# V28 in the rows of w_o, V27 and K31: one ring tile, another layout of w_down's last rows and a copy in three pieces

## The chip, the cores and the metric

The kernel runs on one core of a Trainium2 chip. The metric is the device time of one execution in microseconds (us); the median over runs is given, and one further execution was profiled. The core has engines that work side by side and meet only at semaphores: PE (TensorE, matrix products; its weight loads are listed as PEld), DVE (VectorE), ACT (ScalarE), POOL (GpSimd) and SP (SyncE, which here issues the loads). Loads from memory run on 16 DMA engines. A load is issued by SP, carries 128 rows, one for each partition of the on-chip memory (SBUF), and its semaphore is counted up when all of it has landed. PE writes to PSUM.

## The reference, cut to what matters

One decoding step with two tokens (B = 2), D = 512. The token is normalized; attention over a window of the last W = 2048 cached positions with 32 heads of 128, and a bilinear gated layer with F = 1376 hidden columns, are added to it:

```python
def _A_ref(x, k_cache, v_cache, wq, wo):
    W = min(4096, max(256, Sk // 4))                       # 2048
    q = (x @ wq).reshape(B, Sq, Hq, Dh)                    # 32 heads of 128
    k, v = k_cache[:, :, Sk - W:, :], v_cache[:, :, Sk - W:, :]
    p = softmax(einsum("bhqd,bhkd->bhqk", q, k) * Dh ** -0.5)
    return einsum("bhqk,bhkd->bhqd", p, v).reshape(B, Sq, Hq * Dh) @ wo

def _B_ref(x, w_gate, w_up, w_down):
    return ((x @ w_gate) * (x @ w_up)) @ w_down

xn = layernorm(x)
return x + _A_ref(xn, ...) + _B_ref(xn, ...)
```

All of it is float32. Each head has its own keys and values, so every byte of the cache window is used once: 32 heads times 2 MB of keys and 2 MB of values, and 25 MB of weights.

## The kernel before, in words

**Layout.** The 2 x 2048 positions of a head are put on 128 partitions (64 for each token), 32 positions each, so the keys of one head are a field of 128 rows of 4096 words (CK, 16 KB a row, 2048 KB in all), and so are its values. The host lays all fields out in one DRAM stream (`laid_out`), in the order in which they are loaded, and each load of `loads()` is one contiguous piece of it with 128 equal rows.

**Groups.** Heads are worked in NG = 8 groups of HG = 4. In iteration `it` the keys of group `it` and the values of group `it - 1` are worked. Group g has three loads: `g.0` (two keys and V of head 4g-4), `g.1` (one key, two V) and `g.2` (w_o's rows of the group before, one V, one key, the next columns of w_q). The loads `g.0`, `g.1` and `g.2` are counted on three semaphores, B0, B1 and B2. Group 0's loads carry the gate, up and part of the w_down weights in the place of V. Behind the last keys come `8.0` (V28), `8.1` (V29, V30), `8.2` (V31), `wo` (w_o's last rows), and `d0`, `d1`, `d2` (w_down's rows). The last key is K31 in `7.2`, which also carries V27 and w_o's rows of group 6.

**Ring.** The loads go into three SBUF tiles (`ring`, widths `TILES`), with a fixed slot for each kind of field (`PLACES`), and a field overwrites the one before it in its slot. `Program.put` finds from the overlapping ranges what an instruction has to wait for, so the load of a field waits for the last reader of what it overwrites. SP issues the loads strictly in the order of the program: a load that waits holds those behind it.

**An iteration.** PE: gather of the group before (`gather`), the query columns (`project`), the spread of the maxima (`spread`, tile `top`), w_o's products (`wo`, into `acc`), then the weighing of four heads (`weigh`, eight products each, into `o_ps`), each behind the load with its V. DVE: for each of four keys a product with the query (`products`) and sums over the head's 128 columns (`sums`), then the maxima, the differences and the denominators. ACT: the exponentials (`weights`, tile `p`) and the copies of `o_ps` to `o_sb`, in two halves, with the semaphores `fold` and `fold2`, for which `gather` waits. PE's instructions stand in a loop whose body is run for all groups; that is why its waits are counts that grow with the iteration (`hold`).

**The tail.** After the last group: `scaled` and `wo` for group 7, the four `ROWS` of w_down (from `d0`) into `acc`; DVE adds the token's row (`acc_sb`); the `STRIPS` of w_down (7 and 8 from `d1`, 9 from `d2`) go into `acc_g` in groups of 128 columns, `add_groups(id4, acc_sb)` adds the rest to them, and DVE copies the result to `o_out`, which SP stores. w_down has 1376 = 10 x 128 + 96 rows; chunk NFC = 10, its last 96 rows, is padded to 128 rows of 512 columns, and worked with the chunks 0, 5 and 6 (`EARLY`) in group 0.

Of the kernel before, what the change touches and what calls it, by code (L numbers as in the profile page):

```python
# [10 lines left out]
P = 128  # L11
# [18 lines left out]
EARLY, ROWS, STRIPS = (0, 5, 6, NFC), (1, 2, 3, 4), (7, 8, 9)  # L30
# [5 lines left out]
def gu_cols(n):  # L36
# [18 lines left out]
def field_at(kind, i):  # L55
    if kind == "wq":
        return PLACES["wq", 0][0], C_WQ + i[1] * FB
    if kind == "wo":
        return 2, i % HG * CO
    if kind == "c":  # L60
        return 2, C_C
    return PLACES[kind, i % HG]


def loads():
# [34 lines left out]
    for name, ids in (("d0", ROWS), ("d1", STRIPS[:-1]), ("d2", STRIPS[-1:])):  # L100
        out[name] = (None, [wd[i] for i in ids])
# [3 lines left out]
def placed():  # L105
# [3 lines left out]
    for name, (_, fields) in loads().items():  # L109
        at, lo, tile = None, None, None  # L110
        for kind, i in fields:
            w = gu_cols(i[2]) if kind == "gu" else WIDTHS[kind]
            if kind == "gu":
                t, c = tile, at
            elif kind == "wd":
                if at is not None:
                    t, c = tile, at
                elif name == "0.2":
                    t, c = 2, HG * CO + CK - len(EARLY) * CO
                else:  # L120
                    t, c = 0, (ROWS + STRIPS).index(i) * CO
            else:
                t, c = field_at(kind, i)
            assert at is None or (t, c) == (tile, at), (name, kind, i, c, at)
            got[kind, i] = (t, c, w)
            lo = c if lo is None else lo
            tile, at = t, c + w
        assert at <= TILES[tile], (name, at)
        spans[name] = (tile, lo, at)
    return got, spans  # L130

# [23 lines left out]
class Program:  # L155
# [74 lines left out]
    def plan(self, looped):  # L230
# [46 lines left out]
        for i, o in enumerate(ops):  # L277
            if o.dma:
# [8 lines left out]
    def emit(self, looped, control):  # L287
# [10 lines left out]
        def give(i, first=None):  # L298
# [10 lines left out]
            if i in at:  # L309
                ins.then_inc(sem[o.tag], 16 if o.dma else 1)  # L310
# [127 lines left out]
def build(nc, stream, x_nat, out):  # L438
    pr = Program(nc)
    pe, dve, act, pool = pr.pe, pr.dve, pr.act, pr.pool  # L440

    ring = [pr.sb(f"step{i}", [P, w]) for i, w in enumerate(TILES)]
    xr = pr.sb("xr", [P, D])
    ones = pr.sb("ones", [P, P])
# [19 lines left out]
    hT = pr.sb("hT", [P, 4, NFB, B])  # L464
    acc_sb = pr.sb("acc_sb", [P, D])
# [12 lines left out]
    got = {key: ring[t][:, c : c + w] for key, (t, c, w) in where.items()}  # L478
    src, pos, tag_of = {}, 0, {}
    for name, (tag, _) in loads().items():  # L480
        t, lo, hi = spans[name]
# [4 lines left out]
    def issue(name):  # L486
        t, lo, hi = spans[name]
        pr.load("SP", ring[t][:, lo:hi], src[name], tag=tag_of[name])
# [352 lines left out]
```

## Time and profile before

| what | value |
|---|---|
| median of 3 runs | 376.26 us (376.07 to 377.44) |
| profiled execution | 375.96 us, span 374.6 us |
| DVE busy | 299.5 us (80% of the span) |
| PE busy | 177.2 us (47%), mean granted clock 0.718 |
| ACT, POOL busy | 18.3 us, 3.0 us |
| moved by DMA | 159.62 MB, mean 426 GB/s over the span |
| loads issued on SP | 20 of 6144 KB, 12 others |

The span goes from the first instruction to the last. Nearly every instruction has the line L139 (the helper that records operations), so rows are told apart by their tiles: `step` is the ring, `o_ps` the weighed values, `gu` the PSUM tile that also takes the gather, `q` the query tile, which at the end takes `acc_g`. PE's float32 products show up as two records each, so a head's eight weighing products are counted as x16.

### The profile page before, as it was taken

How to read it: one execution, taken by the hardware profiler on the slowest of the kernel's cores; microseconds unless marked ns; L12 is line 12 of the kernel's file. 1: busy time of each engine (PE TensorE's matmuls, PEld its weight loads, DVE VectorE, ACT ScalarE, POOL GpSimd, SP SyncE). 2: the span in 40 equal slices, each digit the busy share in tenths (PEclk: the TensorE clock that was granted, in tenths of full speed). 3: DMA queues.
4: the chain of work that ended last, by engine and by line, in shares of the span. 5: the costliest groups of instructions: out<-in, count | busy, mean ns of one | idle time of the engine just before them, and what ended most of it. 6: DMA issues, size and time to landing. Idle time of an engine off the chain costs nothing.

```text
span 374.6 us, 2080 instructions
## 1 busy us (share of the span) xinstructions
PE 177.2 (47%) x850; PEld 54.9 (15%) x850; DVE 299.5 (80%) x151; ACT 18.3 (5%) x42; POOL 3.0 (1%) x16
## 2 busy tenths in 40 slices
PE   0664743337516184073923277061740645334876
PEld 0210121002101030010400032010300112010322
DVE  0089999998599796997699975997969976999911
ACT  4000200000000000000000000000000000000000
POOL 3000000000000000000000000000000000000000
PEclk9965859587855688565695858567965659656899
DMA  9999999999999999999999999999999999989996
GB/s 365 415 457 408 444 420 420 457 467 420 420 420 420 430 493 420 420 420 420 425 462 457 420 420 420 420 441 483 420 420 420 420 425 472 446 382 431 439 411 275
DMA packets 4756, 159.62 MB, mean 426 GB/s; under 512 B 530, under 2 KB 658, under 8 KB 916
## 3 DMA queue, kind: packets, MB, share of 16 engines
q1 hardware_dynamic: 4752, 159.62, 98.9%
q10 hardware_dynamic: 4, 0.00, 0.0%
HBM read 159.55 MB, written 0.07 MB: 426 GB/s over the span
## 4 chain that ended last, share of the span: by engine, by line
DMA 50%; DVE 47%; PE 2%; issue 0%; SPq 0%; DVEq 0%
DMA step<-in_stream_dram 50%; DVE step L139 23%; DVE s L139 22%; PE q L139 2%; DVE rs L139 1%; SPq L139 0%; PE acc L139 0%; DVE h_sb L139 0%; PE top L139 0%; DVE nm L139 0%; DVE o_out L139 0%; DVE mt L139 0%; DVE dg L139 0%; DVE mtt L139 0%; DVE mc L139 0%
## 5 line engine op out<-in xcount | busy, mean ns | idle before, releaser
L139 DVE TENSOR_TENSOR step<-step,q 128x4096 f32<-128x4096 f32 x32 | 141.3, 4416 | 41.2 <-DMA step<-in_stream_dram 41.2
L139 PE MATMUL o_ps<-step,p 128*32 128x512 f32 x512 | 93.7, 884 | 156.2 <-DMA step<-in_stream_dram 153.7
L139 DVE TENSOR_REDUCE s<-step 128x32 f32<-128x4096 f32 x32 | 141.4, 4418 | 0.8
L139 PEld LDWEIGHTS o_ps<-step,p 128*32 128x32 f32 x512 | 18.7, 147 | 218.4 <-DMA step<-in_stream_dram 170.6
L139 PE MATMUL q<-step,xnb 128*128 128x512 f32 x72 | 42.0, 736 | 9.0 <-DVE step L139 6.3
L139 PEld LDWEIGHTS q<-step,xnb 128*128 128x128 f32 x72 | 16.5, 241 | 28.2 <-issue 18.2
L139 PE MATMUL gu<-step,xn 128*2 128x512 f32 (+1 forms) x48 | 14.8, 786 | 11.4 <-DMA step<-in_stream_dram 11.4
L139 ACT COPY o_sb<-o_ps 128x256 f32<-128x256 f32 x16 | 5.2, 375 | 247.3 <-PE o_ps L139 247.3
L139 PE MATMUL gu<-step,o_sb 128*128 128x8 f32 x64 | 10.1, 285 | 4.0 <-ACT o_sb L139 4.0
L139 PEld LDWEIGHTS gu<-step,o_sb 128*128 128x128 f32 x64 | 9.4, 225 | 16.5 <-ACT o_sb L139 16.5
L139 ACT ACTIVATE p<-s,zero 64x128 f32<-64x128 f32 x16 | 6.4, 399 | 63.5 <-DVE s L139 63.4
L139 PE MATMUL acc<-step,oT 128*2 128x512 f32 x64 | 8.3, 592 | 0.4 <-DVE oT L139 0.4
L139 DVE TENSOR_REDUCE nm<-top 64x4 f32<-64x8 f32 x16 | 2.6, 164 | 7.0 <-PE top L139 6.9
L139 DVE RECIPROCAL rec<-tot 128x8 f32<-128x8 f32 x8 | 1.6, 199 | 6.2 <-PE tot L139 6.2
L139 PEld LDWEIGHTS gu<-step,xn 128*2 128x2 f32 x48 | 2.9, 99 | 23.2 <-DMA step<-in_stream_dram 13.1
L139 PE MATMUL top<-dg,ones 128*128 128x16 f32 x16 | 2.9, 258 | 6.6 <-DVE dg L139 6.6
L139 DVE TENSOR_REDUCE st<-xc 128x4 f32<-128x16 f32 x1 | 0.2, 169 | 6.2 <-POOL xc L139 6.2
L139 DVE TENSOR_TENSOR oT<-gu,rec 128x8 f32<-128x8 f32 x8 | 1.3, 157 | 4.3 <-PE gu L139 4.3
L139 PEld LDWEIGHTS top<-dg,ones 128*128 128x128 f32 x16 | 2.5, 188 | 12.5 <-DVE dg L139 11.4
L139 DVE TENSOR_REDUCE rs<-p 128x8 f32<-128x256 f32 x8 | 3.3, 414 | 0.9 <-ACT p L139 0.9
L139 ACT ACT_TABLE_LOAD x3 | 3.8, 1283 | 3.1 <-POOL xr L139 3.1
L139 PE MATMUL top<-st,mean_w 128*128 128x4 f32 x2 | 0.6, 364 | 6.4 <-DVE st L139 6.4
(44 smaller groups left out, 31.9 us busy)
## 6 DMA issues: line engine op xcount, KB each, us to landing
step<-in_stream_dram SPq DMA_DIRECT2D x20, 6144.0 KB, 30.4
step<-in_stream_dram SPq DMA_DIRECT2D x2, 4096.0 KB, 23.7
step<-in_stream_dram SPq DMA_DIRECT2D x1, 6080.0 KB, 18.8
step<-in_stream_dram SPq DMA_DIRECT2D x1, 5568.0 KB, 31.5
step<-in_stream_dram SPq DMA_DIRECT2D x1, 5120.0 KB, 29.8
step<-in_stream_dram SPq DMA_DIRECT2D x2, 2048.0 KB, 22.0
step<-in_stream_dram SPq DMA_DIRECT2D x2, 1024.0 KB, 11.6
step<-in_stream_dram SPq DMA_DIRECT2D x1, 1057.0 KB, 4.9
```

Of the source, the lines that this page charges most:

```text
L139: return getattr(engine, self.method)(*self.args, **self.kw)
```

## The change

1. **One ring tile.** The three tiles become one, `step`, of 36992 words a partition, and the slots are ordered anew: V1, V2, K2; w_q, w_o, V3, K3, V0, K0, K1 (the numbers are those within a group). Each load's fields stand in the order of the slots.
2. **V28 in `7.2`.** In the new order V0's slot follows K3's, so `7.2` is extended by V28: its rows are w_o's rows of group 6, V27, K31 and V28 (14336 words instead of 10240). `8.0` is gone. As V28's slot holds V24 until that is weighed, the issue of `7.2` moves behind `weigh(vs[0])` of iteration 7. The count on B0 that `8.0` gave is given by a memset on POOL that waits for `7.2`.
3. **w_down.** Chunk 10 becomes 128 rows of 384 columns: 96 rows as they are, and below them the last 128 columns of these rows as 32 rows of three pieces. It moves to the `STRIPS` (in `d1`, with chunk 8), chunk 7 takes its place in `EARLY`. `rest()` works it: three pairs of products, one with 96 rows and one with 32, the latter with `h3`, to which ACT copies the hidden columns in group 0.
4. **Copies in three pieces.** `o_ps` is copied to `o_sb` in 128, 128 and 256 columns, with three semaphores, and `gather` waits for each before the product that reads it.

The diff, cut to its core:

```diff
@@ -27,7 +27,8 @@
 M = 4 * N
 CK, CO, CQ = J * DH, D, HG * DH
 CX = B * NC + 4 * N + 4 * HG + 2 * NFB + 2 + B
-EARLY, ROWS, STRIPS = (0, 5, 6, NFC), (1, 2, 3, 4), (7, 8, 9)
+EARLY, ROWS, STRIPS = (0, 5, 6, 7), (1, 2, 3, 4), (NFC, 8, 9)
+REST = 3 * P
 GU = [(w, c, n) for w in range(2) for c in range(NC) for n in range(NFB)]
 GU_A = [(0, c, n) for c in range(NC) for n in (2, 0)] + [(0, 0, 1)]
 GU_B = [t for t in GU if t not in GU_A]
@@ -41,25 +42,37 @@
 
 
 
+
+C_WQ = 3 * CK + P
+C_WO = C_WQ + NC * FB
+C_V3 = C_WO + HG * CO
+C_K3 = C_V3 + CK
+C_V0 = C_K3 + CK
+C_K0 = C_V0 + CK
+RING = C_K0 + 2 * CK
 PLACES = {
-    ("k", 0): (0, 0), ("k", 1): (0, CK), ("v", 0): (0, 2 * CK),
-    ("k", 2): (1, 0), ("v", 1): (1, CK), ("v", 2): (1, 2 * CK),
-    ("wo", 0): (2, 0), ("v", 3): (2, HG * CO), ("k", 3): (2, HG * CO + CK),
-    ("wq", 0): (2, HG * CO + 2 * CK),
+    ("v", 1): 0, ("v", 2): CK, ("k", 2): 2 * CK,
+    ("v", 3): C_V3, ("k", 3): C_K3, ("v", 0): C_V0,
+    ("k", 0): C_K0, ("k", 1): C_K0 + CK,
 }
-C_WQ = HG * CO + 2 * CK
-C_C = C_WQ + NC * FB
-TILES = (3 * CK, 3 * CK, C_C + CX)
 
 
 def field_at(kind, i):
     if kind == "wq":
-        return PLACES["wq", 0][0], C_WQ + i[1] * FB
+        return C_WQ + i[1] * FB
     if kind == "wo":
-        return 2, i % HG * CO
+        return C_WO + i % HG * CO
     if kind == "c":
-        return 2, C_C
+        return C_WQ - CX
+    if (kind, i) == ("k", HG - 1):
+        return C_V3
     return PLACES[kind, i % HG]
+
+
+def width(kind, i):
+    if kind == "gu":
+        return gu_cols(i[2])
+    return REST if (kind, i) == ("wd", NFC) else WIDTHS[kind]
 
 
 def loads():
@@ -72,33 +85,33 @@
         return [("v", h) for h in ids]
 
     def wq(g):
-        return [("wq", (g, c)) for c in range(NC)]
+        return [("wq", (g, c)) for c in range(NC)] if g < NG else []
 
     def wo(g):
         return [("wo", h) for h in range(g * HG, g * HG + HG)]
 
+    def wd(*ids):
+        return [("wd", i) for i in ids]
+
     gu_a, gu_b = [("gu", t) for t in GU_A], [("gu", t) for t in GU_B]
-    wd = {i: ("wd", i) for i in range(NFC + 1)}
     out = {
-        "x": ("B2", wq(0) + [("c", 0)]),
-        "0.0": ("B0", k(0, 1) + gu_a),
-        "0.1": ("B1", k(2) + gu_b),
-        "0.2": ("B2", [wd[i] for i in EARLY] + k(3) + wq(1)),
+        "x": ("B2", [("c", 0)] + wq(0)),
+        "0.0": ("B0", gu_a + k(0, 1)),
+        "0.1": ("B1", gu_b + k(2)),
+        "0.2": ("B2", wq(1) + wd(*EARLY) + k(3)),
     }
     for g in range(1, NG):
         a, b = g * HG, g * HG - HG
-        out[f"{g}.0"] = ("B0", k(a, a + 1) + v(b))
-        out[f"{g}.1"] = ("B1", k(a + 2) + v(b + 1, b + 2))
-        out[f"{g}.2"] = (
-            "B2", wo(g - 1) + v(b + 3) + k(a + 3) + (wq(g + 1) if g + 1 < NG else [])
-        )
+        out[f"{g}.0"] = ("B0", v(b) + k(a, a + 1))
+        out[f"{g}.1"] = ("B1", v(b + 1, b + 2) + k(a + 2))
+        out[f"{g}.2"] = ("B2", wq(g + 1) + wo(g - 1) + v(b + 3) + k(a + 3))
     b = H - HG
-    out[f"{NG}.0"] = ("B0", v(b))
+    out[f"{NG - 1}.2"][1].extend(v(b))
     out[f"{NG}.1"] = ("B1", v(b + 1, b + 2))
     out[f"{NG}.2"] = ("B2", v(b + 3))
     out["wo"] = (None, wo(NG - 1))
     for name, ids in (("d0", ROWS), ("d1", STRIPS[:-1]), ("d2", STRIPS[-1:])):
-        out[name] = (None, [wd[i] for i in ids])
+        out[name] = (None, wd(*ids))
     return out
 
 
...
@@ -275,7 +284,7 @@
         places = {ops[j].place for j in wanted if ops[j].eng == "PE" and ops[j].tag == "PE"}
         at, value = {}, {}
         for i, o in enumerate(ops):
-            if o.dma:
+            if o.dma or o.tag in PARTS:
                 step = 16
             elif o.tag in self.tags or i in wanted or (o.eng == "PE" and o.place in places):
                 step = 1
@@ -307,7 +316,7 @@
             if w:
                 ins._wait_ge(*w[-1])
             if i in at:
-                ins.then_inc(sem[o.tag], 16 if o.dma else 1)
+                ins.then_inc(sem[o.tag], 16 if o.dma or o.tag in PARTS else 1)
 
         sections = {}
         for i, o in enumerate(ops):
@@ -439,8 +448,9 @@
     pr = Program(nc)
     pe, dve, act, pool = pr.pe, pr.dve, pr.act, pr.pool
 
-    ring = [pr.sb(f"step{i}", [P, w]) for i, w in enumerate(TILES)]
+    ring = pr.sb("step", [P, RING])
     xr = pr.sb("xr", [P, D])
+    none = pr.sb("none", [P, 1])
     ones = pr.sb("ones", [P, P])
     mean_w = pr.sb("mean_w", [P, P])
     eps_t = pr.sb("eps", [P, 1])
...
@@ -613,10 +624,9 @@
 
     def gather(g):
         pr.part("g")
-        pr.hold("fold", g + 3, "r")
         for r in range(4):
-            if r == 2:
-                pr.hold("fold2", g + 3, "r")
+            if r < 3:
+                pr.hold(f"fold{r}", g + 3, "r")
             pe.matmul(
                 pk_ps[:, 0:N], o_sb[:, r * DH : (r + 1) * DH], pick[:, r, :],
                 start=(r == 0), stop=(r == 3),
@@ -640,8 +650,22 @@
         n_grp += 1
 
     def down(c, add, *args, **kw):
-        k = min(P, F - c * P)
-        add(hT[:k, c % 4, c // 4, :], got["wd", c][:k], *args, **kw)
+        add(hT[:, c % 4, c // 4, :], got["wd", c], *args, **kw)
+
+    def rest():
+        nonlocal n_grp
+        k, w = F - NFC * P, got["wd", NFC]
+        for j in range(3):
+            part = slice(j * P, (j + 1) * P)
+            pe.matmul(
+                acc_g[32 * j : 32 * j + B, :], hT[:k, NFC % 4, NFC // 4, :], w[:k, part],
+                start=(n_grp == 0), stop=False,
+            )
+            pe.matmul(
+                acc_g[96 : 96 + B, :], h3[k:, j, :], w[k:, part],
+                start=(n_grp == 0 and j == 0), stop=False,
+            )
+        n_grp += 1
 
     def wo(g):
         pr.part("o")
...
@@ -691,9 +715,9 @@
             weights(g)
             if it >= 2:
                 wo(g - 1)
-        if it < NG:
+        if it < NG - 1:
             issue(f"{it}.2")
-        else:
+        elif it == NG:
             for name in ("wo", "d0", "d1", "d2"):
                 issue(name)
         ks = [it * HG + hh for hh in range(HG)] if it < NG else []
@@ -703,6 +727,10 @@
             pr.hold("p", it + 1, "r")
             pr.hold("B0", it + 1, "r16")
             weigh(vs[0])
+        if it == NG - 1:
+            issue(f"{it}.2")
+            pr.also = [got["v", H - HG]]
+            pool.memset(none, 0.0, tag="B0")
         if ks:
             products(ks[0])
         if vs:
@@ -711,7 +739,8 @@
             sums(ks[0])
             products(ks[1])
             sums(ks[1])
-            issue(f"{it + 1}.0")
+            if it < NG - 1:
+                issue(f"{it + 1}.0")
         if vs:
             pr.hold("B1", it + 1, "r16")
             weigh(vs[1])
@@ -728,6 +757,10 @@
             sums(ks[2])
             if it == 0:
                 act.copy(hT.rearrange("p i n b -> p (i n b)"), hT_ps[:, 0 : 4 * B * NFB])
+                n = (NFC % 4 * NFB + NFC // 4) * B
+                for j in range(3):
+                    act.copy(h3[96:, j, :], hT_ps[32 * j : 32 * j + 32, n : n + B],
+                             tag=f"fold{j}" if j else None)
                 pr.section, pr.step = "gu", len(GU) + 4
                 for j, i in enumerate(EARLY):
                     down(i, add_rows, j, first=True)
@@ -735,8 +768,8 @@
         if vs:
             pr.hold("B2", it + 2, "r16")
             weigh(vs[3])
-            for n, half in enumerate((slice(0, FB // 2), slice(FB // 2, FB))):
-                act.copy(o_sb[:, half], o_ps[:, half], tag=("fold", "fold2")[n])
+            for n, part in enumerate((slice(0, P), slice(P, 2 * P), slice(2 * P, FB))):
+                act.copy(o_sb[:, part], o_ps[:, part], tag=f"fold{n}")
         if it == NG - 1:
             issue(f"{NG}.2")
         if ks:
@@ -750,7 +783,7 @@
         down(i, add_rows, j, last=True)
     dve.tensor_tensor(acc_sb, acc, xr, op=ALU.add)
     for i in STRIPS[:-1]:
-        down(i, add_groups)
+        rest() if i == NFC else down(i, add_groups)
     add_groups(id4, acc_sb)
     down(STRIPS[-1], add_groups, last=True)
     dve.tensor_copy(o_out, acc_g)
@@ -802,7 +835,12 @@
         if kind == "wo":
             return wo[i]
         if kind == "wd":
-            return np.pad(wd[i * P : (i + 1) * P], ((0, max(0, (i + 1) * P - F)), (0, 0)))
+            if i < NFC:
+                return wd[i * P : (i + 1) * P]
+            w = wd[i * P :]
+            return np.concatenate(
+                [w[:, :REST], w[:, REST:].reshape(3, 32, P).transpose(1, 0, 2).reshape(32, REST)]
+            )
         w, c, n = i
         return gu[w][:, c, n * FB : min(n * FB + FB, F)]
 
```

More of the change, by code (lines that the diff above doesn't have):

```diff
@@ L109, in placed @@
     for name, (_, fields) in loads().items():
[L110 to L119, printed above, removed]
-                else:
[L121 to L129, printed above, removed]
+        fixed = [n for n, (kind, _) in enumerate(fields) if kind not in ("gu", "wd")]
+        if fixed:
+            at = field_at(*fields[fixed[0]]) - sum(width(*f) for f in fields[: fixed[0]])
+        else:
+            late = ROWS + STRIPS
+            at = C_K0 + sum(width("wd", i) for i in late[: late.index(fields[0][1])])
+        lo = at
+        for n, (kind, i) in enumerate(fields):
+            assert n not in fixed or at == field_at(kind, i), (name, kind, i, at)
+            got[kind, i] = (at, width(kind, i))
+            at += width(kind, i)
+        assert at <= RING, (name, at)
+        spans[name] = (lo, at)
     return got, spans
+PARTS = ("B0", "B1", "B2")
 class Op:
@@ L477, in build @@
     where, spans = placed()
-    got = {key: ring[t][:, c : c + w] for key, (t, c, w) in where.items()}
+    got = {key: ring[:, c : c + w] for key, (c, w) in where.items()}
     src, pos, tag_of = {}, 0, {}
     for name, (tag, _) in loads().items():
-        t, lo, hi = spans[name]
+        lo, hi = spans[name]
         src[name] = stream[pos : pos + P * (hi - lo)].rearrange("(p i) -> p i", p=P)
@@ L514, in build @@
         act.activation(t, ones[:, 0:1].to_broadcast([P, FB]), AF.Copy, scale=0.0,
-                       tag="fold" if t is acc else "fold2")
+                       tag=f"fold{(acc, *gu_ps).index(t)}")
     xd, sq = xc[:, 0], xc[:, 1]
```

10 lines of the change are left out of this document (5 added, 5 removed).

## The prediction, made before the changed kernel was run

> **What bounds the kernel now.** I read the page first, then the timeline of the last 60 us, then the DMA issues and stages of the granted clock. The page says which resource is full:
>
> ```profile
> span 374.6 us, 2080 instructions
> q1 hardware_dynamic: 4752, 159.62, 98.9%
> ```
>
> One queue keeps the 16 DMA engines busy for 98.9% of the span, so up to the last group the transfers set the pace, and an edit off that queue costs nothing there. The end is another stage. In the timeline below (start, duration, engine, operation; in brackets the idle time before it and what ended it) each row ended by a DMA gives the landing of one load.
>
> ```profile
> 315.89 6.83 SPq L139 DMA_DIRECT2D step<-in_stream_dram  x2
> 319.01 4.42 DVE L139 TENSOR_TENSOR step<-step,q 128x4096 f32<-128x4096 f32 x1 [3.44 <-DMA step<-in_stream_dram]
> 319.03 3.30 PE L139 MATMUL o_ps<-step,p 128*32 128x512 f32 x16 [3.20 <-DMA step<-in_stream_dram]
> 333.56 0.20 PEld L139 LDWEIGHTS o_ps<-step,p 128*32 128x32 f32 x8 [12.62 <-DMA step<-in_stream_dram]
> ...
> 345.56 0.20 DVE L139 RECIPROCAL rec<-tot 128x8 f32<-128x8 f32 x1
> 345.68 4.42 DVE L139 TENSOR_TENSOR step<-step,q 128x4096 f32<-128x4096 f32 x1
> 345.69 0.20 PEld L139 LDWEIGHTS o_ps<-step,p 128*32 128x32 f32 x8 [5.64 <-DMA step<-in_stream_dram]
> ...
> 350.13 4.42 DVE L139 TENSOR_REDUCE s<-step 128x32 f32<-128x4096 f32 x1
> 350.73 3.68 PE L139 MATMUL q<-step,xnb 128*128 128x512 f32 x8
> ...
> 355.66 0.40 PE L139 MATMUL top<-dg,ones 128*128 128x16 f32 x2 [1.26 <-DVE dg L139]
> 355.99 1.04 PE L139 MATMUL acc<-step,oT 128*2 128x512 f32 x8
> ...
> 356.80 0.81 ACT L139 ACTIVATE p<-s,zero 64x128 f32<-64x128 f32 x2 [6.76 <-DVE s L139]
> ...
> 357.72 0.19 PEld L139 LDWEIGHTS o_ps<-step,p 128*32 128x32 f32 x8 [1.63 <-issue]
> 357.75 1.92 PE L139 MATMUL o_ps<-step,p 128*32 128x512 f32 x16 [0.72 <-ACT p L139]
> 360.29 0.16 PEld L139 LDWEIGHTS o_ps<-step,p 128*32 128x32 f32 x8 [1.52 <-DMA step<-in_stream_dram]
> 360.30 3.64 PE L139 MATMUL o_ps<-step,p 128*32 128x512 f32 x32 [0.62 <-DMA step<-in_stream_dram]
> 360.75 0.13 PEld L139 LDWEIGHTS o_ps<-step,p 128*32 128x32 f32 x4 [0.30 <-issue]
> 361.18 0.13 PEld L139 LDWEIGHTS o_ps<-step,p 128*32 128x32 f32 x4 [0.30 <-issue]
> ...
> 363.86 0.30 PEld L139 LDWEIGHTS tot<-rs,ones 128*128 128x128 f32 x2 [0.84 <-issue]
> ...
> 365.20 1.92 PE L139 MATMUL o_ps<-step,p 128*32 128x512 f32 x16 [0.94 <-DMA step<-in_stream_dram]
> ...
> 367.19 0.65 ACT L139 COPY o_sb<-o_ps 128x256 f32<-128x256 f32 x2 [9.58 <-PE o_ps L139]
> 367.61 1.06 PE L139 MATMUL gu<-step,o_sb 128*128 128x8 f32 x8 [0.49 <-ACT o_sb L139]
> ...
> 369.03 1.04 PE L139 MATMUL acc<-step,oT 128*2 128x512 f32 x8 [0.36 <-DVE oT L139]
> 370.18 1.04 PE L139 MATMUL acc<-step,hT 128*2 128x512 f32 x8
> 371.29 0.69 DVE L139 TENSOR_TENSOR acc_sb<-acc,xr 128x512 f32<-128x512 f32 x1 [2.31 <-PE acc L139]
> 371.46 0.62 PE L139 MATMUL q<-step,hT 128*2 128x128 f32 x16 [0.24 <-DMA step<-in_stream_dram]
> ...
> 372.72 0.29 DVE L139 COPY o_out<-q 128x128 f32<-128x128 f32 x1 [0.74 <-PE q L139]
> ```
>
> Read it as landings: 7.0 at 319.03 (V24 with K28, K29), 7.1 at 333.56, 7.2 at 345.69 (K31, V27), 8.1 at 360.29 (V29, V30), 8.2 at 365.20 (V31). V28 (8.0) shows no waiter: its bytes lie between 345.69 and 360.29. The one tie that matters is at 345.68. DVE had worked without a stop since 319 and finished its `rec` at 345.76; the load with K31 landed in the same tenth. From there runs the last compute chain: product K31, its sums, maxima, `top`, Exp, weighing V28 at 357.75, V29 and V30, V31, gather, w_o, the sum and the store. Only in its PE part does it wait for loads.
>
> **The change part by part.**
>
> *V28 in load 7.2.* Rows of 40 KB become rows of 56 KB, and 8.0 goes. DVE's product of K31 waits for the whole load, so it now waits for V28's 2048 KB also. Sizes (count, KB each, us from issue to landing):
>
> ```profile
> step<-in_stream_dram SPq DMA_DIRECT2D x20, 6144.0 KB, 30.4
> ...
> step<-in_stream_dram SPq DMA_DIRECT2D x1, 5120.0 KB, 29.8
> ...
> step<-in_stream_dram SPq DMA_DIRECT2D x1, 1057.0 KB, 4.9
> ```
>
> Let r be the time of 1024 KB and f what a load costs beside its bytes. 7.1: f + 6r = 333.56 - 319.03 = 14.53. 7.2: f + 5r = 12.13. 8.0 with 8.1: 2f + 6r = 14.60. 8.2: f + 2r = 365.20 - 360.29 = 4.91. The first two give r = 2.40, the others f of 0.07 to 0.11. V28 therefore adds 2r = 4.80, and K31 lands at 350.5 instead of 345.69. DVE has nothing else: everything behind that product on its queue (sums of K31, oT, maxima, weights) is late with it. Bounds 4.7 to 4.9 (a third of 14.60 is 4.87). I take **+4.80**.
>
> [...]
>
> *The issue of 7.2 moves behind the weighing of V24*, whose slot it overwrites. SP issued 7.2 at 315.89 and then stood for 8.0; now 7.2 goes out when the weighing ends, 319.03 + 3.30 = 322.33. The engines are then busy with 7.1 until 333.56: 11 us of cover. Behind it on SP stand 8.1, 8.2, w_o's last rows and the w_down loads. 8.2 waits for V27's weighing, 4.8 late, about 354; 8.1 keeps the engines until about 360. w_o's rows wait for the w_o products of the group before, 357.03 + 4.8 = 361.8, with 8.2 in flight until about 365. No hole is left, **0**; one of 2 us would still lie ahead of where PE now needs these rows.
>
> *POOL's memset that signals B0* runs once 7.2 has landed, at 350.5, with nothing behind it on POOL. PE asks for it at 362.5: **0**. Without those 12 us of cover it would be its own duration, about the 0.10 of this row:
>
> ```profile
> 2.41 0.10 POOL L139 MEMSET zero<- 128x1 f32 x1
> ```
>
> *What the late chain no longer waits for.* Shifted by 4.8, weighing V28 starts at 362.55. V29, V30 have landed and V31 lands during it. Weight loads go 0.43 apart per four (360.75, 361.18), so 16 take 1.71: V29's could have begun at 357.72 + 1.71 = 359.43 and began at 360.29, a wait of 0.86; V31's could have begun 0.30 after `tot`'s at 363.86, a wait of about 1.03. PE's own brackets say 0.62 + 0.94 = 1.56. Between 1.56 and 1.89 I take **-1.75**. w_down's first rows came 0.11 late too (369.03 + 1.04 = 370.07 against 370.18): **-0.11**.
>
> *Copies in three pieces.* By form, the ACT rows are:
>
> ```profile
> L139 ACT COPY o_sb<-o_ps 128x256 f32<-128x256 f32 x16 | 5.2, 375 | 247.3 <-PE o_ps L139 247.3
> L139 ACT COPY hT<-gu 128x24 f32<-128x24 f32 x1 | 0.2, 180 | 4.9 <-PE gu L139 4.9
> ```
>
> On the line between them 128 columns take 267 ns, so gather may start 0.11 earlier; its third product comes 0.53 later and finds its piece. Bounds 0 (PE waits for the later pieces) and -0.13: **-0.10**, once, at the end; in other groups DMA hides it.
>
> *w_down's last 96 rows.* 64 KB fewer are 64/1024 x 2.40 = 0.15, but in a stream that now ends before its users. In the tail strips 7 and 8 were 8 products, 16 in the trace, which shows each twice; now `rest()` has 6 and strip 8 has 4, so 20. The 16 took 0.62 beside `acc_sb` (0.69), so 20 take 0.78; PE's next step waits from the end of the rows' products for 0.07 + 0.69 + 0.06 = 0.82 anyway: **0**, bounds 0 and +0.16. The three small copies to h3, by the 0.18 of the 24-column copy, run in the first group on an ACT with nothing due before the first Exp: **0**; uncovered they are 0.54.
>
> *The order of fields inside other rows and the single tile* change no length and no wait of the loads through 7.1: **0**.
>
> Sum: 4.80 - 1.75 - 0.11 - 0.10 = **+2.84**; from ends 4.7 - 1.89 - 0.11 - 0.13 = 2.6 and 4.9 - 1.56 + 0.16 = 3.5. The profiled execution took 375.96 with a span of 374.6; it becomes 378.8. The median of the runs is 0.30 above it, so 376.26 + 2.84 = **379.1**.
>
> **The rivals.**
>
> *The granted clock halves during the last weighing.* Stages of 3.41 us (behind the times stand the length and PE's busy time; third from the end is the clock):
>
> ```profile
> 270.67:274.09 3.42, 1.37 (x10) 0.40 (x10) 0.77 (x4) 0.80 (x2) 0.00 (x0) 1.00 1.06 460
> 274.09:277.50 3.41, 2.06 (x12) 0.59 (x16) 2.08 (x1) 0.00 (x0) 0.00 (x0) 0.50 1.07 461
> 352.59:356.01 3.42, 2.16 (x11) 0.83 (x12) 2.91 (x6) 0.00 (x0) 0.00 (x0) 1.00 0.89 383
> 356.01:359.42 3.41, 2.69 (x25) 0.58 (x24) 1.04 (x4) 0.80 (x2) 0.00 (x0) 1.00 0.90 389
> ```
>
> After a stage with 40% PE work the clock fell to 0.50, after one with 63% it held. Between project (ends 354.41) and the weighing (357.75) lie 3.34 us with 1.37 of work, 41%; before, two stages shared them. Shifted by 4.8, one stage may lie just over them. It holds less than 1.7 of work, half of itself, if it begins between 0.33 ahead of project's end (0.33 + 1.37) and 0.26 behind it (1.37 + 0.07 + 0.26): 0.6 of 3.41 us. The next stage would do half its work: +1.7, **380.8**. Against it: four in five positions.
>
> [...]
>
> *A load costs much beside its bytes, and merging saves it.* The lone first load (1057 KB) took 4.9 from issue to landing, 2.4 more than its bytes at r. If each load in line paid that, one load fewer would take 2.84 - 2.3 = 0.5: **376.8**. Against it: four landings agree on f near 0.1, and engines 98.9% busy have no room for 2.4 in each of some 30 loads. [...]
>
> *Not slower: K31's load lands early enough.* The place is 7.2, 7168 KB from 333.56. If K31 landed by 350.5 - 2.84 = 347.65, the chain would end as before, and the saved bytes and load would leave about 376.26 - 0.25 = **376.0**. That needs 7168 KB in 14.1 us, where 6144 took 14.53. [...]
>
> **How the numbers follow.** About 0.5%, 1.9 us, is what a measurement of this kernel can tell from no change. Chances: forecast 0.66 (its own range 378.7 to 379.9), halved clock 0.18, load cost 0.05, not slower 0.06, something unnamed 0.05 to either side. Slower: 0.66 + 0.18 + half of the unnamed, 0.86; within 0.5% 0.11; faster 0.03. The range takes the forecast and most of the clock's case: 378.3 to 381.0.
>
> **What would show it.** In the new profile: DVE idle about 4.7 us, ended by a DMA, ahead of the last product at about 350.5; the last Exp near 361.6; the last four weighings in about 7.9 us with no wait for a DMA; PE work from the w_down strips not waiting for a DMA; DMA empty for its last 5 us or so. A last product that starts before 348 would make the forecast wrong, and so would a hole in the DMA row between 333 and 365, or a granted clock of 0.50 after 360.

## The result, and the profile after

The changed kernel takes **381.25 us** (median of 6 runs, 379.9 to 381.93) beside 376.28 for the kernel before (6 runs, 376.07 to 377.44). The ratio is 1.0124, with a 95% interval of 1.0099 to 1.0149: slower by 1.0% to 1.5%, and 2.15 us above the forecast of 379.1. The direction was right; the size was not, and the runs spread over 2.0 us. The forecast's range ended at 381.0: three of the six runs lie inside it and three above, the median 0.25 above. The measured ratio, put on the 376.26 that the forecast started from, gives 380.9, just below that end.

The profiled execution took 381.78. Its page, sections on the span and the queue:

```profile
span 380.4 us, 2100 instructions
...
q1 hardware_dynamic: 4608, 159.55, 97.5%
```

The span grew by 5.8 us, and the queue carries 144 packets fewer. The timeline of its last 62 us (start, duration, engine, operation, in brackets the idle time before it and what ended it):

```profile
322.81 43.24 SPq L148 DMA_DIRECT2D step<-in_stream_dram  x7
...
333.66 5.91 PE L148 MATMUL o_ps<-step,p 128*32 128x512 f32 x32 [10.91 <-DMA step<-in_stream_dram]
...
350.58 4.42 DVE L148 TENSOR_TENSOR step<-step,q 128x4096 f32<-128x4096 f32 x1 [4.74 <-DMA step<-in_stream_dram]
350.60 3.64 PE L148 MATMUL o_ps<-step,p 128*32 128x512 f32 x16 [10.71 <-DMA step<-in_stream_dram]
...
354.63 1.88 PE L148 MATMUL gu<-step,o_sb 128*128 128x8 f32 x8 [0.39 <-ACT o_sb L148]
...
356.35 6.57 PE L148 MATMUL q<-step,xnb 128*128 128x512 f32 x8
...
360.28 0.23 DVE L148 TENSOR_SCALAR dg<-step,mc 128x16 f32<-128x16 f32 x1
...
362.76 0.29 PE L148 MATMUL top<-dg,ones 128*128 128x16 f32 x2
...
363.79 0.81 ACT L148 ACTIVATE p<-s,zero 64x128 f32<-64x128 f32 x2 [8.77 <-DVE s L148]
...
364.74 5.36 PE L148 MATMUL o_ps<-step,p 128*32 128x512 f32 x48 [0.72 <-ACT p L148]
...
370.35 1.92 PE L148 MATMUL o_ps<-step,p 128*32 128x512 f32 x16
...
372.65 1.06 PE L148 MATMUL gu<-step,o_sb 128*128 128x8 f32 x8 [0.39 <-ACT o_sb L148]
...
374.07 1.04 PE L148 MATMUL acc<-step,oT 128*2 128x512 f32 x8 [0.36 <-DVE oT L148]
...
374.93 1.04 PE L148 MATMUL acc<-step,hT 128*2 128x512 f32 x8
...
375.79 0.38 PE L148 MATMUL q<-step,hT 96*2 96x128 f32 x2
...
376.04 0.69 DVE L148 TENSOR_TENSOR acc_sb<-acc,xr 128x512 f32<-128x512 f32 x1 [2.02 <-PE acc L148]
376.10 0.38 PE L148 MATMUL q<-step,h 32*2 32x128 f32 x2
...
377.63 0.40 PE L148 MATMUL q<-step,hT 128*2 128x128 f32 x8
...
377.85 0.40 PE L148 MATMUL q<-acc_sb,step 128*2 128x128 f32 x8
```

Each of these times is set against the same row of before, which is in the prediction or among these rows of before:

```profile
345.70 3.62 PE L139 MATMUL o_ps<-step,p 128*32 128x512 f32 x16 [5.55 <-DMA step<-in_stream_dram]
...
349.81 1.06 PE L139 MATMUL gu<-step,o_sb 128*128 128x8 f32 x8 [0.50 <-ACT o_sb L139]
...
372.04 0.40 PE L139 MATMUL q<-acc_sb,step 128*2 128x128 f32 x8
```

| place | before | after | late by | step |
|---|---|---|---|---|
| DVE's product of K31 | 345.68 | 350.58 | 4.90 | +4.90 |
| weighing of V28 | 357.75 | 364.74 | 6.99 | +2.09 |
| end of V31's weighing | 367.12 | 372.27 | 5.15 | -1.84 |
| gather | 367.61 | 372.65 | 5.04 | -0.11 |
| w_down's rows (`acc` from `hT`) | 370.18 | 374.93 | 4.75 | -0.29 |
| `q` from `acc_sb` | 372.04 | 377.85 | 5.81 | +1.06 |

Four steps are the forecast's in their sign and, but for w_down's rows, in their size. Two are not: +2.09 ahead of the weighing and +1.06 in the strips. In the first, DVE is on time: `dg` ends at 360.51, but `top` comes 2.25 later, since the query products (`project`) take 6.57 instead of 3.68 and gather 1.88, where the one at 372.65 takes 1.06. The stages of the changed kernel say why (behind the times: length, busy time of PE, PEld, DVE, ACT, POOL, then the granted clock, the DMA share and GB/s):

```profile
352.40:355.80 3.40, 3.02 (x18) 1.28 (x10) 3.37 (x2) 0.71 (x3) 0.00 (x0) 0.50 0.90 386
355.80:359.20 3.40, 3.40 (x8) 1.85 (x8) 3.40 (x1) 0.00 (x0) 0.00 (x0) 0.50 1.00 429
359.20:362.60 3.40, 3.40 (x6) 1.40 (x5) 1.21 (x6) 0.00 (x0) 0.00 (x0) 0.56 0.95 405
```

PE works from 350.60 on, and the clock stays at 0.50 until about 362.2 (0.56 in the last row means that 0.12 of that stage was at full clock). Before, the stages at the same piece of the chain were these:

```profile
345.77:349.18 3.41, 3.41 (x16) 0.52 (x16) 3.41 (x1) 0.00 (x0) 0.00 (x0) 0.50 0.94 399
349.18:352.59 3.41, 2.91 (x17) 1.82 (x14) 3.38 (x2) 0.65 (x2) 0.00 (x0) 1.00 1.23 529
```

There the weighing of V27 (345.70 to 349.32), at half clock too, filled one stage, and the next had the full clock, just in time for gather (1.06) and `project` (3.68).

### The profile page after: what moved, and what is told of

Its sections match the earlier page's. It is cut to its first block, busy times and chain, and to the rows that moved or that the text cites. A ratio compares the mean times of both kernels' runs of the same rounds, so it can differ in the third digit from the quotient of the medians.

```text
span 380.4 us, 2100 instructions
## 1 busy us (share of the span) xinstructions
PE 180.7 (48%) x854; PEld 58.5 (15%) x854; DVE 299.5 (79%) x151; ACT 19.2 (5%) x53; POOL 3.1 (1%) x17
## 4 chain that ended last, share of the span: by engine, by line
DMA 53%; DVE 38%; PE 8%; issue 0%; ACT 0%; SPq 0%; DVEq 0%
DMA step<-in_stream_dram 53%; DVE s L148 19%; DVE step L148 18%; PE o_ps L148 4%; PE q L148 2%; PE gu L148 1%; DVE rs L148 1%; PE acc L148 0%; ACT p L148 0%; DVE h_sb L148 0%; DVE nm L148 0%; PE top L148 0%; ACT o_sb L148 0%; SPq L148 0%; PE tot L148 0%
## 5 line engine op out<-in xcount | busy, mean ns | idle before, releaser
L148 PE MATMUL o_ps<-step,p 128*32 128x512 f32 x512 | 91.4, 865 | 160.8 <-DMA step<-in_stream_dram 158.4
L148 PE MATMUL q<-step,xnb 128*128 128x512 f32 x72 | 46.2, 799 | 8.7 <-DVE step L148 6.0
L148 PEld LDWEIGHTS q<-step,xnb 128*128 128x128 f32 x72 | 18.1, 264 | 30.7 <-issue 20.7
L148 PE MATMUL gu<-step,xn 128*2 128x512 f32 (+1 forms) x48 | 13.7, 737 | 12.4 <-DMA step<-in_stream_dram 12.4
L148 ACT COPY o_sb<-o_ps 128x128 f32<-128x128 f32 (+1 forms) x24 | 5.7, 309 | 249.6 <-PE o_ps L148 249.6
L148 PEld LDWEIGHTS gu<-step,o_sb 128*128 128x128 f32 x64 | 11.0, 259 | 15.8 <-ACT o_sb L148 15.8
L148 PE MATMUL gu<-step,o_sb 128*128 128x8 f32 x64 | 11.7, 311 | 3.1 <-ACT o_sb L148 3.1
```

Source lines behind the costliest of these rows:

```text
L148: return getattr(engine, self.method)(*self.args, **self.kw)
```

## The experiments

Each is an edit of the changed kernel unless it says otherwise; "before" is the kernel before on the same chip; "..." stands for lines of an edit that are left out. The theory: V28's bytes, about 2.8; `rest()`, about 1; the clock, the rest of it, different from run to run.

**e1_unmerge: V28 in a load of its own again, all else kept.**

```diff
-    out[f"{NG - 1}.2"][1].extend(v(b))
+    out[f"{NG}.0"] = ("B0", v(b))
...
-        if it < NG - 1:
+        if it < NG:
             issue(f"{it}.2")
...
-        if it == NG - 1:
-            issue(f"{it}.2")
-            pr.also = [got["v", H - HG]]
-            pool.memset(none, 0.0, tag="B0")
...
-            if it < NG - 1:
-                issue(f"{it + 1}.0")
+            issue(f"{it + 1}.0")
```

> The changed kernel with V28 back in a load of its own (8.0), issued where it was before; the one ring tile, w_down's new rows and the copies in three pieces stay. Theory (V28's bytes hold back K31, the rest of the loss is in the tail): the last product starts at about 345.8 again, the last weighing waits for DMA again, and the time is 376.3 plus what w_down's rows cost in the tail, about 1.1: 377.2 to 377.6. Rival (the one tile, the slot order or the rows cost it): it stays above 379.5.

Measured: 377.38 (10 runs, 377.29 to 379.75) beside 376.02; ratio 1.0044 (1.0025 to 1.0064). Eight of the ten lie between 377.29 and 377.51; why two are at 379.6 and 379.75 stays open. Timeline of e1, of a run of the eight:

```profile
345.66 4.41 DVE L148 TENSOR_TENSOR step<-step,q 128x4096 f32<-128x4096 f32 x1
...
351.43 5.47 PE L148 MATMUL q<-step,xnb 128*128 128x512 f32 x8
...
365.18 1.92 PE L148 MATMUL o_ps<-step,p 128*32 128x512 f32 x16 [0.79 <-DMA step<-in_stream_dram]
...
371.30 0.38 PE L148 MATMUL q<-step,hT 96*2 96x128 f32 x2
...
373.15 0.40 PE L148 MATMUL q<-step,hT 128*2 128x128 f32 x8
```

K31 is worked at 345.66 again. `project` ran slowly here too (5.47), and it cost nothing, since PE waits for V31 at 365.18, as before at 365.20: that landing had been the cover over PE's clock. What stays is `rest()`: 1.85 from 371.30 to 373.15, of which 1.3 lies on the path (`q` from `acc_sb` starts at 373.36, before at 372.04).

**e2_oldrows: chunk 10 as 96 rows of 512 columns, four products; V28 still in `7.2`.**

```diff
-    return REST if (kind, i) == ("wd", NFC) else WIDTHS[kind]
+    return WIDTHS[kind]
...
-        rest() if i == NFC else down(i, add_groups)
+        down(i, add_groups)
...
```

> The changed kernel, but chunk 10 of w_down comes again as 96 rows of 512 columns padded to 128 and is worked in d1 by four products of 96 rows in four column groups; V28 stays in 7.2. Theory (the pairs of 96- and 32-row products take 0.31 each, 1.9 where a strip takes 0.3): the products between the rows of w_down and acc_sb's are hidden beside acc_sb again, the time falls by about 1.06 against the changed kernel's 381.25: 379.2 to 380.6, spread as wide as before by the granted clock. Rival (PE waits there for acc_sb and d1 anyway): no fall, 381.2.

Measured: 379.45 (4 runs, 378.45 to 380.73) beside 376.02; ratio 1.0077 (1.0054 to 1.01). Timeline of e2:

```profile
356.29 6.66 PE L148 MATMUL q<-step,xnb 128*128 128x512 f32 x8
...
374.96 1.04 PE L148 MATMUL acc<-step,hT 128*2 128x512 f32 x8
375.81 0.62 PE L148 MATMUL q<-step,hT 96*2 96x128 f32 x16
...
376.81 0.40 PE L148 MATMUL q<-acc_sb,step 128*2 128x128 f32 x8 [0.37 <-DVE acc_sb L148]
```

The strips now end inside `acc_sb`, and PE waits for DVE as it did before. `q` from `acc_sb` starts 1.85 behind w_down's rows (374.96), in the changed kernel 2.92: `rest()` costs 1.07. The medians differ by 1.8, but both kernels spread over 2 us. The clock's loss is still there (`project` takes 6.66), and so is the spread.

**e3_reorder: `rest()` with its three 96-row products first, then the three 32-row ones.**

```diff
                 start=(n_grp == 0), stop=False,
             )
+        for j in range(3):
+            part = slice(j * P, (j + 1) * P)
             pe.matmul(
                 acc_g[96 : 96 + B, :], h3[k:, j, :], w[k:, part],
```

> The changed kernel with rest() in another order: the three products of 96 rows first, then the three of 32 rows. If each change between the row strips 0 to 95 and 96 to 127 costs, two changes stay instead of six: rest() takes about 0.7 instead of 1.86 and is hidden beside acc_sb, time down by 0.9 to 1.06. If it is that the three products of 32 rows go into one column group one after the other, rest() takes about 1.2 (0.3 + 3 x 0.31), time down by 0.5. If the number of products counts alone, no change.

Measured: 380.37 (4 runs, 378.84 to 381.04) beside 376.02; ratio 1.0097 (1.0066 to 1.0128). The median is 0.9 lower, within a spread of 2 us; the timeline of e3 shows the gain apart from the spread:

```profile
375.84 0.40 PE L148 MATMUL q<-step,hT 96*2 96x128 f32 x6
...
376.17 0.81 PE L148 MATMUL q<-step,h 32*2 32x128 f32 x6
...
376.91 0.40 PE L148 MATMUL q<-step,hT 128*2 128x128 f32 x8
```

The same six products take 1.07 (375.84 to 376.91) instead of 1.84 (375.79 to 377.63). In the changed kernel every product, alternating between the two shapes, cost 0.31. Here the 96-row ones take 0.33 together, but the 32-row ones 0.74, 0.25 each, though nothing changes between them. The new order has four changes of the shape fewer and takes 0.77 less, some 0.19 for each; that is not the whole of the 1.84. Why the 32-row products are slow one after the other is not shown; they differ from the fast ones in their rows and in that all three go into the same 32 columns. Nor does a run show what happens at a change of the shape.

**e4_noproj: no query products in the iteration behind the last keys, where their result is not used; the output stays complete.** If late query products held `top`, taking them away would free it.

```diff
-        project(it)
+        if it < NG:
+            project(it)
```

> The changed kernel without the query products that PE runs once more in the iteration after the last keys; their result is not used, so no output is left out. Theory (in the profiled run these eight records ran at the halved clock, 6.57 instead of 3.68, and held the spread of the maxima by 2.2): the spread starts when DVE is ready, at about 360.5, in every run. But PE is then idle from 356.5 to 360.5, so the weighing may start at the halved clock and lose 1.7 to 3.4: 379 to 382, and the Exp near 361.6. Rival (the clock is not what holds the spread): the spread still starts near 362.8 and the time stays at 381.3.

Measured: 381.76 (4 runs, 381.68 to 381.85) beside 376.02; ratio 1.0147 (1.0128 to 1.0165). No gain. The timeline of e4:

```profile
360.64 0.61 PE L148 MATMUL top<-dg,ones 128*128 128x16 f32 x2 [4.06 <-DVE dg L148]
...
362.95 7.23 PE L148 MATMUL o_ps<-step,p 128*32 128x512 f32 x48
...
370.43 1.92 PE L148 MATMUL o_ps<-step,p 128*32 128x512 f32 x16
```

`top` does come with `dg`, 2.1 earlier, but PE has stood for 4.06, and V28 to V30 are weighed at half clock, 7.23 instead of 5.36: V31's weighing starts at 370.43, as in the changed kernel (370.35). The query products had been late, but with them the clock rose at 362.17 (in the changed kernel), without them only at 366.8. The spread is gone too, 0.17 us; why all four executions agree so closely, though the clock's rise (at 366.8 in the profiled one) could fall elsewhere in the weighing, stays open. The stages of e4 (columns as above) have 0.50 in the gap and in the two stages behind it:

```profile
356.50:359.90 3.40, 0.08 (x1) 0.00 (x0) 3.37 (x4) 0.00 (x0) 0.00 (x0) 0.50 0.95 405
359.90:363.30 3.40, 2.65 (x14) 0.83 (x18) 1.66 (x7) 0.80 (x2) 0.00 (x0) 0.50 0.97 414
363.30:366.70 3.40, 3.40 (x20) 0.90 (x16) 0.00 (x0) 0.00 (x0) 0.00 (x0) 0.50 0.91 328
```

**e5_early: V28 in its own load, and chunk 10 in its short form (384 columns, the 32 rows apart) worked in group 0; one tile, the order of the slots and the copies kept.**

```diff
-EARLY, ROWS, STRIPS = (0, 5, 6, 7), (1, 2, 3, 4), (NFC, 8, 9)
+EARLY, ROWS, STRIPS = (0, 5, 6, NFC), (1, 2, 3, 4), (7, 8, 9)
...
-    out[f"{NG - 1}.2"][1].extend(v(b))
+    out[f"{NG}.0"] = ("B0", v(b))
...
```

> V28 in a load of its own, and chunk 10 of w_down, in its shorter form, worked with chunks 0, 5 and 6 in the first group (one product of 96 rows over 384 columns, three of 32 rows over the last 128), so that nothing of it is left in the tail; the copies in three pieces and the one tile stay. Theory (the two losses are V28 ahead of K31 and the pairs of products in the tail, and nothing else in the change costs): both are gone and the time is that of the kernel before less the 64 KB, 375.8 to 376.3 beside 376.0. Rival (slot order or the copies have a cost of their own): above 376.6.

Measured: 375.93 (12 runs, 375.76 to 377.04) beside 376.11 (17 runs); ratio 0.9994 (0.9984 to 1.0004): no difference. The parts not undone here cost nothing that can be measured. `project` took 5.44 in its profile, again without effect.

**e8_v28first: V28 as a load of its own, but issued directly ahead of `7.2`; no memset, no long rows.** It tells V28's bytes from the merging.

```diff
...
         if it == NG - 1:
+            issue(f"{NG}.0")
             issue(f"{it}.2")
-            pr.also = [got["v", H - HG]]
-            pool.memset(none, 0.0, tag="B0")
```

> V28 in a load of its own, 8.0, but issued directly ahead of 7.2, both behind the weighing of V24; no memset on POOL. Theory (the price is V28's bytes ahead of K31 on the queue, not the longer row, the memset or the later issue): K31's product starts at about 350.6 as in the changed kernel and the time is as there, 380 to 382. Rival (a load with rows of 56 KB or a semaphore through POOL is what costs): K31 at about 346, 377.4.

Measured: 381.2 (4 runs, 379.99 to 382.42) beside 376.11; ratio 1.0117 (1.0093 to 1.014), as the changed kernel. Timeline of e8:

```profile
334.24 5.87 PE L148 MATMUL o_ps<-step,p 128*32 128x512 f32 x32 [10.89 <-DMA step<-in_stream_dram]
...
351.25 4.42 DVE L148 TENSOR_TENSOR step<-step,q 128x4096 f32<-128x4096 f32 x1 [4.80 <-DMA step<-in_stream_dram]
```

DVE waits 4.80 (this run was 0.6 late from its first loads). The two loads, 8.0 and `7.2`, landed 17.01 behind 7.1 (334.24 to 351.25), where the one long load of the changed kernel took 16.92. What counts is that 2048 KB stand ahead of K31, in the same load or in the one before it.

**e6_warm, e7_warm_oldrows: ten dummy products per key group behind the third weighing** (a tile that nothing reads), to hold the clock up; e7 with e2's rows besides. **e9_warm_last, e10_warm_last_oldrows, e11_early_warm: eleven of them, in the last key group alone**; e10 with e2's rows, e11 on e5. In all five the products are written out one by one; the core of e9:

```diff
...
+    with nc.body("pe_warm", valid_engines=only):
...
+        for _ in range(11):
+            pe.matmul(warm_ps, xnb[:, 0, :], xnb.rearrange("p c k -> p (c k)"),
+                      start=True, stop=True)
+        pe.br("pe_w2")
...
```

> The changed kernel with ten products more on PE in each group, behind the sum of the denominators and ahead of the wait for the third load, into a PSUM bank that nobody reads; the last iteration has none. PE is then busy while it would wait for 7.2. Theory (PE comes out of the 10.7 us wait for 7.2 at the halved clock, and the query products at 6.5 instead of 3.7 hold the spread of the maxima): the query products take about 3.7, the spread starts near 360.5, the time falls by about 2.1 to 378.9 to 379.5, and the runs spread by less than 0.8. Rival (these products are slow because DVE or the loads use the same memory): still 6.5, time 381.3 or more.

> The same ten products, and chunk 10 of w_down in the old padded form, worked in d1 by four products of 96 rows. What is left is V28 ahead of K31 alone. The prediction's sum for that, with the terms as the profile shows them: 4.9 late, 1.84 and 0.3 of waits for loads gone, 0.1 by the copies, +2.7 on 376.0: 378.4 to 379.0. If a further loss is in the change: above 379.5.

> The changed kernel with eleven products more on PE in the last group with keys only, between the sum of the denominators and the wait for 7.2, into a PSUM bank that nobody reads. [...] Theory (the halved clock behind the wait for 7.2 holds the query products): they take about 3.7, or end before DVE is ready, the spread starts near 360.5, time 378.9 to 379.6, runs within 0.8 of each other. Rival (the clock has no part in it): 381.3 and the spread of the changed kernel.

> The same eleven products, and chunk 10 of w_down in the old padded form. What is left is V28 ahead of K31 alone: 4.9 late, 1.84 and 0.3 of waits for loads gone, 0.1 by the copies: +2.7 on the kernel before's 376.1, 378.3 to 379.0. A further loss in the change would show as more than 379.3.

> V28 in a load of its own, chunk 10 worked in the first group, and the eleven products while PE waits for 7.2. By the theory the slack behind K31 (1.75) already hides the halved clock in most runs of this order, so the median stays at 375.8 to 376.1; what should go are the single runs near 377, in which the query products at the halved clock hold the spread by more than the slack. Rival (those runs have another cause): they stay, about one in five.

| run | median, range | beside | ratio (95%) | K31 product | `project` |
|---|---|---|---|---|---|
| e6 | 381.57, 381.32 to 381.87 | 376.11 | 1.0139 (1.0122 to 1.0157) | 351.89 | 5.40 |
| e7 | 381.04, 380.58 to 382.32 | 376.11 | 1.0119 (1.0102 to 1.0136) | 351.85 | 6.73 |
| e9 | 381.48, 381.27 to 381.62 | 376.08 | 1.0133 (1.0111 to 1.0154) | 351.82 | 3.68 |
| e10 | 380.64, 380.23 to 381.01 | 376.08 | 1.0111 (1.0088 to 1.0133) | 352.21 | 5.29 |
| e11 | 378.14, 377.72 to 378.68 | 376.08 | 1.0044 (1.0027 to 1.0061) | 347.08 | 3.68 |

Misses, all of them, for two reasons. In e6, e7 and e10 the clock was down again when `project` ran (5.40, 6.73 and 5.29), though only in e7 did that hold up `top`. And in all five K31 came late. The page's queues and the timeline of e9:

```profile
q8 instruction: 2, 0.03, 0.0%
```

```profile
339.51 9.69 PE L452 MATMUL warm<-xnb 128*128 128x512 f32 x22
351.82 4.42 DVE L148 TENSOR_TENSOR step<-step,q 128x4096 f32<-128x4096 f32 x1 [5.97 <-DMA step<-in_stream_dram]
...
356.57 3.68 PE L148 MATMUL q<-step,xnb 128*128 128x512 f32 x8
...
361.81 0.39 PE L148 MATMUL top<-dg,ones 128*128 128x16 f32 x2 [1.56 <-DVE dg L148]
```

Here `project` is fast and `top` waits for DVE, as wanted, but K31 landed 1.24 later. A queue of instructions has appeared, with two packets (0.03 MB), which the changed kernel does not have; the pages of e6 and e11 have the same line. In e9 and e10 `7.2` landed 18.17 and 18.45 behind 7.1, instead of 16.92. e11 paid the same: its product of K31 waited 1.38 for the load, where e5's waited for none. In e6 and e7, `7.2` took its 16.92, and the 1.3 by which K31 came late (351.89 and 351.85 against 350.58) had come in the first group, where PE stood before its w_down products for no wait that the profile shows (3.58 in e6, 4.92 in e7). That the packets hold up a load under way, or PE, was the author's guess; the runs show only that the two come together.

**e12_loop_oldrows: the dummies as a loop around one product, with e2's rows.** The code is short now; the run asks whether the queue of instructions and the late load go with that.

```diff
...
+    with nc.body("pe_warm", valid_engines=only):
...
+        pe.matmul(warm_ps, xnb[:, 0, :], xnb.rearrange("p c k -> p (c k)"),
+                  start=True, stop=True)
+        pe.reg_add(c, c, 1)
+        pe.br_lt(c, 12, on_true="pe_warm", on_false="pe_w3")
...
```

> As the kernel with eleven products and the old form of chunk 10, but the products run in a loop of one, so that the program is hardly longer; in the unrolled ones an instruction queue appears among the DMA queues (2 packets) and the load under way lands 1.3 late. Theory (V28 ahead of K31 is the whole of what is left, the halved clock and the pairs of products being gone): no instruction queue, K31's product at about 350.6, spread of the maxima at about 360.6, and 376.1 + 4.9 - 1.84 - 0.3 - 0.1 = 378.8; 378.3 to 379.1, runs within 0.8. Rival (the 1.3 came from the products' reads beside the load): K31's product near 351.8 again and 380 or more.

Measured: **378.6** (5 runs, 378.55 to 378.75) beside 376.1; ratio 1.0067 (1.0053 to 1.0081). The queue of instructions is gone from its page. Timeline of e12:

```profile
350.67 4.42 DVE L148 TENSOR_TENSOR step<-step,q 128x4096 f32<-128x4096 f32 x1 [4.73 <-DMA step<-in_stream_dram]
...
355.15 3.70 PE L148 MATMUL q<-step,xnb 128*128 128x512 f32 x8 [1.09 <-DVE step L148]
...
360.66 0.40 PE L148 MATMUL top<-dg,ones 128*128 128x16 f32 x2 [1.81 <-DVE dg L148]
...
362.75 5.36 PE L148 MATMUL o_ps<-step,p 128*32 128x512 f32 x48 [0.72 <-ACT p L148]
...
374.79 0.40 PE L148 MATMUL q<-acc_sb,step 128*2 128x128 f32 x8 [0.37 <-DVE acc_sb L148]
```

This is the forecast's chain: K31 4.99 later, `top` behind DVE, the weighing 5.00 later (357.75 to 362.75), `q` from `acc_sb` 2.75 later (372.04 to 374.79). With the clock held and `rest()` away, the change costs 2.5 by the medians, and the spread falls from 2.0 to 0.2. The kernel before has little to gain from such dummies on its last chain: its `top` waits 1.26 for DVE, and its last weighings ran at full clock; the dummies were not run in it. None of these kernels beats the one before.

## Why the prediction was wrong in its size

**K31's landing, +4.80: right.** 4.90 in the changed kernel, 4.99 in e12. `7.2` landed 16.92 behind `7.1` (333.66 to 350.58); f + 7r was 16.9. e1 takes it away by moving V28 behind K31 again, e8 brings it back without the long load.

**The waits that vanish, -1.75: right.** -1.84: four weighings in 7.53 (364.74 to 372.27), no row with a DMA. **w_down's rows, -0.11: too small.** -0.29, since the products of `acc` from `oT` and from `hT` follow at 0.86 (374.07 to 374.93), not at the 1.04 of the row's busy time that I added. **Copies, -0.10: right** (-0.11). **Memset, later issue, one tile and slots, 0: right.** The memset ran at 350.67; `7.2` went out at 322.81, and its load was not late for it. e5 has no difference.

**w_down's last rows at 0: the step that failed, +1.06.** The prediction let 20 records take 0.78, by 0.62 for 16, and hid them under `acc_sb`. The 0.62 is the time of strips that all have the same rows and go to four different places of 32 columns. `rest()` alternates between 96 and 32 rows; its twelve records took 1.84, strip 8 follows, and `acc_sb` had ended at 376.73. The bound of +0.16 counted products and not their shapes. No row of before showed an alternation, so that bound should not have been drawn from rows of one shape. e2 removes the term (1.07 in the traces), e1 shows it with little else (ratio 1.0044). e3 splits it: 0.77 of the 1.84 goes with the order, which has four changes of the shape fewer.

**"Everything behind that product ... is late with it": failed for PE, +2.09 in the profiled run.** The prediction moved `top` by 4.80 with DVE, and so took for granted that PE's gather and `project` keep up. They had a margin of 1.26 and a duration of 3.68 from the last group alone. The page of before had the group's row:

```profile
L139 PE MATMUL q<-step,xnb 128*128 128x512 f32 x72 | 42.0, 736 | 9.0 <-DVE step L139 6.3
```

42.0 over nine groups is 4.67 a group: 3.68 was a fast case. At half clock `project` started 0.72 later than its shift (356.35 against 350.73 + 4.90), behind the slow gather, and took 2.89 more; less the 1.26, `top` should be 2.35 late, and was 2.20 (362.76 against 360.56).

**The clock's rival: right in kind, wrong in place.** It let the clock fall in the last weighing, at +1.7. The weighing ran at full clock (5.36 for 48 records). It was ahead of it that the clock had not risen. The trace shows where the clock changed: read in stages of 0.4 us, its 36 changes all lie, within 0.01 us, on one grid of 3.413 us. The last changes are a fall at 341.70 and the rise at 362.17, six steps later; three of the edges between are 351.93, 355.35 and 358.76. V27's weighing, 350.60 to 354.24, lies across the first of these. In the four stages up to 362.17 PE was busy for 1.33, 3.04, 3.41 and 3.41 us; 0.72 of the second and 1.15 of the third were gather. Only behind the fourth, which `project` alone filled, did the clock rise. In the kernel before, V27's weighing fills the stage from 345.74 to 349.15 (3.41 of 3.41), and the clock rises at its end.

The trace of before agrees: its 38 changes lie on a grid of 3.413 us too, with an edge at 349.15 where the changed kernel has one at 348.52. In these two traces, from 80 us on, full clock followed each of the 29 stages at half clock in which products other than gather's filled 0.82 or more of them, and none of the 78 in which they filled 0.74 or less; no stage lay between. So what these two executions paid went with where their edges lay; what sets the edges is not shown. That they may lie anywhere, from which the prediction had its four in five positions, was the author's estimate, and so was the border of one half, between the 40% and 63% of its two rows. That the same makes the 2 us of spread among the runs that were not profiled is argued; for it speaks e12, where the clock stays at 1.00 from 339.7 to the end of the weighings, and the spread falls to 0.2. That 380.8 came near 381.25, and the range's end with it, is luck: the range was widened for a loss in the last weighing, which did not come, and held no more than 0.16 for `rest()`.

By the medians: 2.5 for V28 with the small terms (e12), about 1.1 for `rest()`, which leaves 4.97 - 2.5 - 1.1 = 1.4 for the clock, from 0.0 (the run at 379.9) to 2.1 (at 381.93). The 1.4 is a remainder. e2 and e12, which differ by the dummies alone, are 0.85 apart by their medians; with four runs of e2 over 2.3 us the two figures do not contradict each other.

**The cost of a load, and not slower: both fell.** e8 has one load more than the changed kernel, and its two loads took 0.09 longer than the one (17.01 and 16.92); the 2.3 us a load that the rival needed do not show. 7168 KB took 16.92, not 14.1.

**The signs named beforehand.** DVE's 4.74 at 350.58 came; the last weighings and strips had no wait for a DMA; no load ran any more from 373 on (DMA share 0.00 in the stages of 1 us from there). The last Exp, said near 361.6, came at 363.79; and a granted clock of 0.50 after 360, named as what would make the forecast wrong, stood until 362.2.

## What to carry to other kernels

Before you shift a chain by one engine's delay, ask of every other engine in it how much margin it has and whether its duration is from a fast case: a group's mean over the whole run beside the last one's duration tells. When a change takes away the waits for transfers, it takes away the cover for all that runs slowly by chance (the clock, +2.09 here) or by its shape (`rest()`, +1.06), so what cost nothing must be priced again without it. And products are not priced by their count alone: look for a row with the same sequence of shapes, or leave the bound open above.

## What the runs showed of the hardware that was not expected

- In the changed kernel six products, of 96 and of 32 rows in turn, took 1.84 at full clock, 0.31 us each; strip 8's four products of one shape, to four places, took 0.22 together (377.63 to 377.85). Three 32-row products in a row, into the same place, took 0.74, 0.25 each (e3).
- In the traces of before and of the changed kernel the 38 and 36 changes of the granted clock lie on a grid of 3.413 us, with edges at 349.15 in the one and at 348.52 in the other.
- In the changed kernel the records show PE busy throughout from 355.35 to 358.76, for 1.15 us of it with gather's products of 8 columns, and behind that stage the clock stayed at 0.50.
- Eleven products written out one by one came with two packets of a queue of instructions (e9, e11), and the load under way landed 1.2 to 1.6 us later (e9, e10, e11); the same products as a loop came with neither (e12).
